# Homes that outlive attention: the first weights and tokens of stage 1 are loaded before attention has ended

## The chip, the cores and the metric

The kernel runs on one core of a Trainium2 chip. The metric is the device time of one execution in microseconds (us), as the median of several runs. One execution was also recorded by the hardware profiler; all rows below come from that recording.

## What is computed

Three parts follow one another, each reading what the one before it wrote:

```python
scores = 1/sqrt(64) * q @ k.T                      # 4 batches, 12 heads, 448 x 448
scores = einsum('bhij,hg->bgij', scores, w_pre)    # heads mixed before the softmax
attn = softmax(scores)
attn = einsum('bhij,hg->bgij', attn, w_post)       # and after it
x = (attn @ v) as 1792 tokens x 768
h = x @ w_in; x = (h - tanh(h)) @ w_out            # d_ff 2048
d, c = softmaxes over columns and rows of x @ phi  # 32 slots, 8 experts
out = c @ experts(d.T @ x)
```

## The kernel before

**Attention** (`talking_heads`) handles 184 slots of up to ten query rows each, numbered 0 to 183. In the loop over slots `s`, even slots run `premix` (product `pm`, line 313), `postmix` of the pair four slots back (product `tm`, line 356, into two PSUM tiles that have no second copy), and `expo` (`e`, line 325); odd slots run `recip`, `norm` (`wk`) and `gather` (copies of `tm` to `aT` on ScalarE, lines 373 and 374). `regroup(s + 4)` (line 304, tile `D`) brings the scores of a coming slot into their place by DMA. Beside them run the key and query transposes, `values` (`vx`, line 395, and its copies to `xs` on VectorE, line 405) and the conversion of the double precision weights `w_in` and `w_out` to fp32 (class `Conversion`, tiles `f64` and `fa`; its last step is an addition on GpSimd, line 71). Every step is written in a fixed order (`manual_schedule`), so the order in the code is the order on each engine's queue.

**Stage 1** (`moe_and_slots`) is a generator, which attention advances with `next(more)`. A unit of weights `w` lies in one half of a tile `rg` or `rgs`, and is split into a high and a low part (`split_w`: ScalarE line 787, VectorE or GpSimd line 788); the tokens `xa` likewise (`split_x`, lines 823 and 824). `save_w` (line 801) stores a split unit to DRAM from ScalarE's DMA queue. `product(t)` is 18 matmuls `hp` (line 840), three for each of six pieces of x. `gate_act`, `gate_first` and `gate_last` then compute `h - tanh(h)` on ScalarE and VectorE. Before `box["go"]`, products 0 and 1 run between attention's last steps; then `step(t)` follows for all others, in four passes over the 16 units.

The seam before: at slot 180 all early tiles of attention are released, and the loads are issued from the queue of SyncE (SP):

```python
    for t in range(4):
        load_w(t)
        if t == 0:
            load_x(0)
    yield
    split_w(0, nc.vector)
    save_w(0)
    idle = bank("h1", [128, 128], "warm")
    for _ in range(5):
        nc.tensor.matmul(idle, lhsT=ident, rhs=ident, start=True, stop=True)
```

The tail of attention then advances the generator after `postmix(180)`, `gather(180)`, `postmix(182)`, `gather(182)`, and after the last three `values`. The DMA of the last `xs` (line 380) is issued from ScalarE.

Of the kernel before, what the change touches and what calls it, by code (L numbers as in the profile page):

```python
# [18 lines left out]
NR = 4  # L19
# [54 lines left out]
class Conversion:  # L74
    def __init__(self, nc, w_in, w_out, wi, wo):
# [6 lines left out]
        self.t = {}  # L82

    def load(self, j):
        f, hf, o = j
        r = self.pool.tile([128, self.CV, 2], I32, tag="f64", name="f64", bufs=self.bufs)
# [46 lines left out]
def talking_heads(tc, ident, q, k, v, w_pre, w_post, xd, box, follow):  # L133
# [18 lines left out]
    cv.pool = er  # L152
    psq = early_stack.enter_context(tc.tile_pool(name="at_psq", bufs=2, space=PSUM))
# [7 lines left out]
    def load_k(b, p):  # L161
        t = er.tile([JP, 2, NR, HD], FP32, tag="kn", name="kn", bufs=NP)
        nc.sync.dma_start(out=t, in_=k[b, 2 * p:2 * p + 2].rearrange("e (p r) d -> p e r d", r=NR))
        nat_k[b, p] = t
# [406 lines left out]
    for a in at.get(("head", -1), []):  # L571
        for f in scores4(*a):
            f()
    halves = []
# [4 lines left out]
    while s < NS:  # L579
# [63 lines left out]
def moe_and_slots(tc, ident, xd, wi, wo, wo4, wis, consts, w1, w2, out, box):  # L643
# [34 lines left out]
    keep = whole.enter_context(tc.tile_pool(name="m_keep", bufs=1, reuse_waits="tile"))  # L678
    rgp = whole.enter_context(tc.tile_pool(name="m_ring", bufs=1, reuse_waits="tile"))
    xap = whole.enter_context(tc.tile_pool(name="m_xa", bufs=1, reuse_waits="tile"))  # L680
    xep = firsts.enter_context(tc.tile_pool(name="m_xe", bufs=1, reuse_waits="tile"))
    ph = psums.enter_context(tc.tile_pool(name="m_h", bufs=1, space=PSUM))
    bank_pool = {"h0": ph, "h1": ph}
# [6 lines left out]

    ceK = keep.tile([128, NBL, NSL], FP32, tag="ceK", name="ceK")
# [4 lines left out]
    rg = rgp.tile([128, 2 * RU], FP32, tag="rg", name="rg")  # L696
    rgs = rgp.tile([128, 2 * RU], FP32, tag="rgs", name="rg")
    xbuf = {0: [xap.tile([128, XW], FP32, tag=f"x{l}", name="xa") for l in range(2)]}
    quad, quad_a, quad_b = [xep.tile([128, FB * NRM], FP32, tag=f"quad{i}", name="quad") for i in range(3)]
    ring = [w.rearrange("p (m h i) -> p m h i", m=2, h=2) for w in (rg[:, :RU], rg[:, RU:], rgs[:, :RU], rgs[:, RU:])]  # L700

    def unit(t):
        return ring[t % 4] if t < THREE else ring[(4, 0, 1)[(t - THREE) % 3]]
# [105 lines left out]
    def load_x(p):  # L809
# [7 lines left out]
        step = KD if p else 2  # L817
        for a in range(0, KD, step):
            nc.sync.dma_start(out=dst[:, a:a + step], in_=xd[p][:, a:a + step])
# [275 lines left out]
    def step(t):  # L1095
# [75 lines left out]
        if b == NPASS - 2 and f == NF - 1:  # L1171
            mem["slow"] = True
            for l in range(2):
                give(xap.tile([128, EXB], FP32, tag=f"x{l}", name="ex"))
# [13 lines left out]
    for t in range(4):  # L1188
# [378 lines left out]
```

## Time and profile before

| what | before |
|---|---|
| time, median of 3 runs | 885.64 us (884.59 to 890.2) |
| the profiled execution | 886.23 us, span 884.5 us |
| busy: PE, DVE, ACT, POOL | 807.9, 556.7, 570.5, 247.7 us |
| granted TensorE clock, mean | 0.988 |
| DMA | 224.53 MB, mean 254 GB/s |

PE is TensorE, DVE VectorE, ACT ScalarE, POOL GpSimd, SP SyncE; "ACTq" and "SPq" are the DMA issues of these engines. In a timeline a row gives the start, the time, the engine, the line, the operation, `out<-in`, shapes and the count; what stands in brackets is the idle time of the engine ahead of it and what ended that. An fp32 matmul of the program stands as two records.

### The profile page before, as it was taken

The numbers are of one execution on the slowest core, as the hardware profiler recorded it, in microseconds if no ns is written. First come the engines' busy times: TensorE is split into PE (matmuls) and PEld (weight loads), VectorE is DVE, ScalarE is ACT, GpSimd is POOL, SyncE is SP. The second block draws the span as 40 slices with busy tenths as digits, with TensorE's granted clock in tenths as the row PEclk, the third lists the DMA queues.
The fourth block names the chain that finished last, engine by engine and source line by source line (L and its number), as shares of the span: only waits on it lengthen the run. The fifth ranks groups of instructions, "written<-read, shape, count | busy, mean of one in ns | idle before, by whom it ended". The sixth has DMA issues, their size and how long they took to land.

```text
span 884.5 us, 28648 instructions
## 1 busy us (share of the span) xinstructions
PE 807.9 (91%) x11790; PEld 570.8 (65%) x11790; DVE 556.7 (63%) x1181; ACT 570.5 (64%) x1345; POOL 247.7 (28%) x428
## 2 busy tenths in 40 slices
PE   8889988799987999899899999999999999999965
PEld 6556665566665667566676667667776786964322
DVE  5357766577666777788456986566765777830104
ACT  4777887687776878798666776546664666821103
POOL 5234344334334444454303452000000003700000
PEclk9999999899999999999999999999999999999988
DMA  9787888768888788785759976678764457899998
GB/s 182 191 234 220 213 236 248 218 190 211 231 253 226 219 206 239 236 254 177 256 176 363 374 260 223 207 316 317 302 215 175 149 179 256 313 359 413 424 392 303
DMA packets 131766, 224.53 MB, mean 254 GB/s; under 512 B 44852, under 2 KB 112436, under 8 KB 128052
## 3 DMA queue, kind: packets, MB, share of 16 engines
q1 hardware_dynamic: 128288, 209.84, 74.8%
q10 hardware_dynamic: 3348, 12.87, 3.7%
q8 instruction: 93, 1.52, 0.7%
q14 instruction: 37, 0.30, 0.1%
HBM read 147.96 MB, written 36.18 MB: 208 GB/s over the span
## 4 chain that ended last, share of the span: by engine, by line
PE 50%; DMA 18%; ACT 13%; DVE 12%; issue 5%; SPq 1%; POOL 1%; ACTq 0%; POOLq 0%; DVEq 0%
PE hp L840 21%; DMA D<-S 7%; DMA ex<-in_moe_w_dram 7%; ACT e L325 6%; PE pm L313 5%; PE sc L279 5%; DVE mx L317 4%; PE vx L395 3%; PE tm L356 3%; PE gt L911 2%; ACT S L287 2%; PE kx L236 2%; PE lgp L995 2%; PE sp L1077 1%; ACT aT L370 1%
## 5 line engine op out<-in xcount | busy, mean ns | idle before, releaser
L325 ACT ACTIVATE e<-pm,mx 128x448 f32<-128x448 f32 x184 | 115.1, 631 | 86.3 <-DVE mx L317 84.9
L840 PE MATMUL hp<-xa,rg 128*128 128x512 f32 x576 | 152.7, 405 | 0.2 <-POOL rg L788 0.2
L317 DVE TENSOR_REDUCE mx<-pm 128x1 f32<-128x448 f32 x184 | 106.1, 618 | 73.5 <-PE pm L313 73.4
L356 PEld LDWEIGHTS tm<-wk,e 64*56 64x56 f32 x5888 | 104.7, 128 | 62.8 <-issue 32.4
L356 PE MATMUL tm<-wk,e 64*56 64x60 f32 x5888 | 113.5, 216 | 13.3 <-issue 7.9
L313 PE MATMUL pm<-D,wpre 64*64 64x448 f32 (+2 forms) x736 | 107.6, 565 | 18.4 <-DMA D<-S 15.2
L840 PEld LDWEIGHTS hp<-xa,rg 128*128 128x128 f32 x576 | 102.3, 188 | 28.9 <-issue 10.5
L287 ACT ACTIVATE S<-sc 120x448 f32<-120x448 f32 (+1 forms) x186 | 91.4, 553 | 4.6 <-PE sc L279 3.0
L279 PE MATMUL sc<-khi,qT 64*120 64x448 f32 (+1 forms) x384 | 83.6, 392 | 9.3 <-DVE xs L405 6.2
L342 POOL TENSOR_SCALAR wk<-wpost,rv 128x60 f32<-128x60 f32 x184 | 86.9, 503 | 16.5 <-DVE rv L335 13.8
L331 POOL TENSOR_SCALAR rv<-ss 128x2 f32<-128x2 f32 x92 | 24.5, 266 | 225.3 <-ACT e L325 194.6
L395 PE MATMUL vx<-aT,vn 128*64 128x120 f32 (+1 forms) x1536 | 83.9, 262 | 2.0 <-ACT S L287 1.3
L797 POOL TENSOR_TENSOR rg<-rg 128x384 fp32r<-128x384 f32 x24 | 23.9, 1012 | 208.8 <-DVE rg L794 205.0
L395 PEld LDWEIGHTS vx<-aT,vn 128*64 128x64 f32 x1536 | 74.7, 137 | 7.2 <-issue 3.0
L860 ACT ACTIVATE sq<-hp 128x512 f32<-128x512 f32 (+1 forms) x62 | 32.9, 530 | 68.0 <-PE hp L840 68.0
L370 ACT ACTIVATE aT<-tm 128x480 f32<-128x480 f32 x144 | 75.8, 593 | 0.1
L871 DVE SCALAR_TENSOR_TENSOR qd<-qd,sq 128x512 f32<-128x512 f32 (+1 forms) x61 | 37.6, 616 | 59.1 <-ACT mk L867 53.7
L840 PE MATMUL hp<-xb,rg 128*128 128x512 f32 x288 | 74.7, 404 | 0.0
L840 PEld LDWEIGHTS hp<-xb,rg 128*128 128x128 f32 x288 | 52.1, 188 | 16.6 <-issue 6.3
L279 PEld LDWEIGHTS sc<-khi,qT 64*120 64x120 f32 (+1 forms) x384 | 45.3, 173 | 26.1 <-PE tm L356 9.4
L71 POOL TENSOR_TENSOR fa<-fa,f 128x384 f32<-128x384 f32 x56 | 57.7, 1030 | 6.4 <-DVE f L66 2.1
L313 PEld LDWEIGHTS pm<-D,wpre 64*64 64x64 f32 (+2 forms) x736 | 23.9, 132 | 51.4 <-DMA D<-S 23.2
(199 smaller groups left out, 1391.3 us busy)
## 6 DMA issues: line engine op xcount, KB each, us to landing
ex<-in_moe_w_dram SPq DMA_DIRECT2D x21, 1536.0 KB
D<-S SPq DMA_DIRECT2D x144, 210.0 KB
rg<-wis SPq DMA_DIRECT2D x36, 768.0 KB
f<-in_moe_w_in_dram SPq DMA_DIRECT2D x32, 384.0 KB
wis<-rg ACTq DMA_DIRECT2D x16, 768.0 KB
f<-in_moe_w_out_dram SPq DMA_DIRECT2D x24, 384.0 KB
rg<-wi SPq DMA_DIRECT2D x19, 384.0 KB
wi<-fa SPq DMA_DIRECT2D x32, 192.0 KB
```

The source lines that it names most:

```text
L71: eng.tensor_tensor(out=out, in0=bits(a), in1=bits(p), op=ALU.add)
L279: nc.tensor.matmul(xs[e][0][:ni], lhsT=qT[n][s, l, p, :ni], rhs=kt[s], start=(i == 0), stop=(i == 2))
L287: nc.scalar.activation(out=dst, in_=xs[e][0][:ni], func=ACTF.Copy)
L313: nc.tensor.matmul(xs[x][64 * i:64 * i + 64], lhsT=wpre[k0:k1], rhs=d[i][k0:k1], start=True, stop=True)
L317: nc.vector.tensor_reduce(out=mx[:, x:x + 1], in_=xs[x], op=ALU.max, axis=AX.X, negate=True)
L325: nc.scalar.activation(out=es[x], in_=xs[x], func=ACTF.Exp, bias=mx[:, x:x + 1], accum_out=ss[:, x:x + 1])
L342: nc.gpsimd.tensor_scalar(out=wk, in0=wpost, scalar1=rv[:, x:x + 1], scalar2=None, op0=ALU.mult)
L356: nc.tensor.matmul(xs[i][64 * z:64 * z + JH, x, c], lhsT=es[x][h, j:j + JH], rhs=wks[x][h], start=True, stop=True)
L370: nc.scalar.activation(out=out[:, :, c0:c0 + m].rearrange("p a (x i) -> p a x i", x=2), in_=x, func=ACTF.Copy)
L395: nc.tensor.matmul(x[64 * e:64 * e + 64, i, :ni], lhsT=nat_v[b, h // NP][:, h % NP, c, :], rhs=a[:, c, h, :ni], start=(c == 0), stop=(c == ...
L840: nc.tensor.matmul(hp, lhsT=r32(w[:, m, hl, cs]), rhs=r32(x_of(b, c, l)), start=(c == 0 and i == 0), stop=(c == KD - 1 and i == 2))
L871: nc.vector.scalar_tensor_tensor(out=qd, in0=qd, scalar=TG_E, in1=sq, op0=ALU.add, op1=ALU.mult)
```

## The change

The tiles of the ring (`rg`, `rgs`) and the tile `xl` for x come from a pool `homes` that is opened outside of both parts. During attention `rgs` holds the natural keys (`kns`) and `xl` four of the five raw buffers of the conversion; `rg` holds nothing. From slot 165 on the generator is advanced at every second slot: four loads of w, then three pieces of x. At slot 182 it splits w unit 0, stores it and splits piece 0 of x; at slot 183 pieces 1 and 2. Products 0 and 1 move one or two advances ahead, and the five warm products are gone.

```diff
+    def place(self, x):
+        n = x.shape[1] // 4
+        self.raw = [x[:, i * n:(i + 1) * n] for i in range(4)]
+        self.raw += [self.pool.tile([128, n], FP32, tag="f64", name="f64", bufs=1)]
     def load(self, j):
-        r = self.pool.tile([128, self.CV, 2], I32, tag="f64", name="f64", bufs=self.bufs)
+        r = self.raw[self.loads % self.bufs].bitcast(I32).rearrange("p (f w) -> p f w", w=2)
+        self.loads += 1
...
+    kns = box["homes"].tile([128, NP * 2 * NR * HD], FP32, tag="rgs", name="kn")
+    cv.place(box["homes"].tile([128, 4 * 2 * cv.CV], FP32, tag="xl", name="f64"))
...
+    first_load = NS - D_AHEAD - 15
...
+        if s == first_load:
+            more = follow()
+        if s >= first_load and (s - first_load) % 2 == 0 and s < first_load + 14:
+            next(more)
         if s == NS - D_AHEAD:
             early_stack.close()
-            more = follow()
+            next(more)
+        if s in (NS - 2, NS - 1):
             next(more)
...
+    for t in range(4):
+        load_first(t)
+        yield
+    xl = rgp.tile([128, XW], FP32, tag="xl", name="xa")
+    for a in range(0, KD, 2):
+        nc.sync.dma_start(
+            out=xl.rearrange("p (a s) -> p a s", a=KD)[:, a:a + 2], in_=xd[0][:, a:a + 2])
+        yield
...
-    for t in range(4):
-        load_w(t)
-        if t == 0:
-            load_x(0)
     yield
     split_w(0, nc.vector)
     save_w(0)
-    idle = bank("h1", [128, 128], "warm")
-    for _ in range(5):
-        nc.tensor.matmul(idle, lhsT=ident, rhs=ident, start=True, stop=True)
-    for i in range(0, KD, 2):
-        for c in range(i, i + 2):
-            split_x(0, c)
-        yield
-        product(0, {}, i, i + 2)
+    split_x(0, 0)
+    yield
+    for c in range(1, KD // 2):
+        split_x(0, c)
+    yield
+    product(0, {}, 0, 2)
+    for c in range(KD // 2, KD):
+        split_x(0, c)
+    yield
+    product(0, {}, 2, 4)
+    yield
+    product(0, {}, 4, KD)
```

ScalarE's queue at slot 182, before: the last exponential, the gather of slot pair 178, then the split and the store of w unit 0.

```order
L325 ACTIVATE e_148,ss_8304<-pm_8263,mx_8268 128x448
L373 ACTIVATE aT_8131<-tm_170 128x48x5
L374 ACTIVATE aT_8131<-tm_170 128x48x4
L373 ACTIVATE aT_8131<-tm_171 128x48x5
L374 ACTIVATE aT_8131<-tm_171 128x48x4
L787 ACTIVATE rg_8222<-rg_8222 128x2x384
L801 DMA wis0_89<-rg_8222 128x1536
L823 ACTIVATE xa_8224<-xa_8225 128x512 x2
```

The same place on ScalarE in the changed kernel (lines are some 30 higher there):

```order
L335 ACTIVATE e_151,ss_8227<-pm_8186,mx_8191 128x448
L816 ACTIVATE rg_7574<-rg_7574 128x2x384
L830 DMA wis0_89<-rg_7574 128x1536
L850 ACTIVATE xa_8155<-xa_7879 128x512
L383 ACTIVATE aT_8067<-tm_173 128x48x5
L384 ACTIVATE aT_8067<-tm_173 128x48x4
L383 ACTIVATE aT_8067<-tm_174 128x48x5
L384 ACTIVATE aT_8067<-tm_174 128x48x4
L850 ACTIVATE xa_8155<-xa_7879 128x512 x5
```

The split of w, its store and the first piece of x have moved ahead of the gather.

VectorE's queue at attention's last values, before (the last pair of copies to `xs`, the split of w unit 2, gate 0):

```order
L405 COPY xs<-vx 128x2x8x9
L405 COPY xs<-vx 128x2x2x8
L788 TENSOR_TENSOR rg<-rg 128x2x384
L871 SCALAR_TENSOR_TENSOR quad<-quad 128x512
L872 SCALAR_TENSOR_TENSOR quad<-quad 128x512
L879 TENSOR_TENSOR g_8453<-hp,g_8453 128x512
L884 SCALAR_TENSOR_TENSOR hp<-quad,hp 128x512
L885 COPY_PREDICATED g_8453<-quad,hp 128x512
```

The same place on VectorE in the changed kernel (splits of w units 1 and 2, gate 0, the first pair of copies):

```order
L817 TENSOR_TENSOR rg<-rg 128x2x384 x2
L898 SCALAR_TENSOR_TENSOR quad<-quad 128x512
L899 SCALAR_TENSOR_TENSOR quad<-quad 128x512
L906 TENSOR_TENSOR g_8366<-hp,g_8366 128x512
L911 SCALAR_TENSOR_TENSOR hp<-quad,hp 128x512
L912 COPY_PREDICATED g_8366<-quad,hp 128x512
L415 COPY xs<-vx 128x2x8x9
L415 COPY xs<-vx 128x2x2x8
```

All six copies to `xs` now stand behind gate 0; before, they stood ahead of it. On TensorE, 12 of product 0's matmuls, then `postmix(182)`, the last 6 and all of product 1 now stand ahead of the last three `values`.

SP's queue at slots 173 to 177, before (regroups `D`, stores of converted weights):

```order
L120 DMA wi15_84<-fa_7646 128x384
L304 DMA D_143<-S_7380 108x1x448
L304 DMA D_144<-S_7380 108x1x448
L304 DMA D_139<-S_7380 108x1x448
L120 DMA wi15_84<-fa_7809 128x384
L304 DMA D_140<-S_7380 108x1x448
```

The same place on SP in the changed kernel:

```order
L127 DMA wi15_84<-fa_7572 128x384
L718 DMA xa_7879<-xd0_65 128x1024
L314 DMA D_146<-S_7307 108x1x448
L314 DMA D_147<-S_7307 108x1x448
L718 DMA xa_7879<-xd0_65 128x1024
L314 DMA D_142<-S_7307 108x1x448
L127 DMA wi15_84<-fa_7739 128x384
```

The first piece of x stands ahead of the regroups of slots 178 and 179. It waits there for GpSimd's addition of the last converted piece, whose raw buffer lies in `xl`.

## Rows read from the trace of the kernel before

**Rows 1.** The page's part 4: shares of the chain that ended last, by engine.

```profile
PE 50%; DMA 18%; ACT 13%; DVE 12%; issue 5%; SPq 1%; POOL 1%; ACTq 0%; POOLq 0%; DVEq 0%
```

**Rows 2.** The chain in order of time, from 560 us: start, us, what.

```profile
804.17 16.60 DMA ex<-in_moe_w_dram
```

**Rows 3.** Timeline of the seam, TensorE: start, us, instructions, idle before them.

```profile
437.48 1.31 PE L356 MATMUL tm<-wk,e 64*56 64x60 f32 x55 [0.20 <-ACT aT L374]
...
441.30 0.36 PE L356 MATMUL tm<-wk,e 64*56 64x60 f32 x9 [2.51 <-issue]
...
441.60 1.38 PE L1197 MATMUL warm<-ident 128*128 128x128 f32 x10
...
442.73 1.64 PE L840 MATMUL hp<-xa,rg 128*128 128x512 f32 x6
...
444.30 1.07 PE L356 MATMUL tm<-wk,e 64*56 64x60 f32 x64
...
448.26 3.86 PE L395 MATMUL vx<-aT,vn 128*64 128x88 f32 x96
452.06 5.73 PE L840 MATMUL hp<-xa,rg 128*128 128x512 f32 x24
...
462.35 0.73 PE L840 MATMUL hp<-xa,rg 128*128 128x512 f32 x2 [0.19 <-POOL rg L788]
```

**Rows 4.** The same timeline, ScalarE, VectorE and GpSimd.

```profile
436.68 0.44 ACT L373 ACTIVATE aT<-tm 128x240 f32<-128x240 f32 x1
...
437.65 0.86 ACT L787 ACTIVATE rg<-rg 128x768 fp32r<-128x768 f32 x1
...
438.54 0.96 DVE L788 TENSOR_TENSOR rg<-rg 128x768 fp32r<-128x768 f32 x1 [0.64 <-ACT rg L787]
439.53 0.35 ACTq L801 DMA_DIRECT2D wis<-rg  x1
...
442.64 2.21 ACT L823 ACTIVATE xa<-xa 128x512 fp32r<-128x512 f32 x4
...
448.71 0.60 ACT L860 ACTIVATE quad<-hp 128x512 f32<-128x512 f32 x1 [1.53 <-PE hp L840]
...
450.44 0.71 ACT L867 ACTIVATE quad<-quad,tlimit 128x512 f32<-128x512 f32 x1
...
452.17 0.49 DVE L405 COPY xs<-vx 128x144 f32<-128x144 f32 x2 [0.74 <-PE vx L395]
452.69 0.62 ACTq L380 DMA_DIRECT2D xd<-xs  x1
453.36 0.85 ACT L787 ACTIVATE rg<-rg 128x768 fp32r<-128x768 f32 x1 [2.20 <-DVE xs L405]
...
455.11 0.68 DVE L871 SCALAR_TENSOR_TENSOR quad<-quad 128x512 f32<-128x512 f32 x1
...
460.45 1.84 POOL L788 TENSOR_TENSOR rg<-rg 128x768 fp32r<-128x768 f32 x1 [22.08 <-ACT rg L787]
```

**Rows 5.** Timelines of regroups: issues on SP, GpSimd's last addition, TensorE's premix.

```profile
41.29 1.68 SPq L304 DMA_DIRECT2D D<-S  x2
...
45.77 0.60 PE L313 MATMUL pm<-D,wpre 64*64 64x448 f32 x3 [2.17 <-DMA D<-S]
...
418.28 3.58 SPq L304 DMA_DIRECT2D D<-S  x3
...
419.91 1.01 POOL L71 TENSOR_TENSOR fa<-fa,f 128x384 f32<-128x384 f32 x1
...
425.76 1.58 PE L313 MATMUL pm<-D,wpre 64*64 64x448 f32 x8 [0.78 <-ACT e L325]
```

**Rows 6.** Windows: length, busy of PE, PEld, DVE, ACT, POOL, PEclk, DMA share, GB/s.

```profile
46.00:50.00 4.00, 4.00 (x82) 3.16 (x75) 2.51 (x6) 2.51 (x7) 0.93 (x3) 0.64 0.83 205
50.00:54.00 4.00, 3.22 (x78) 1.50 (x74) 2.10 (x5) 2.43 (x8) 1.07 (x5) 0.93 1.06 214
...
442.00:444.00 2.00, 2.00 (x15) 1.76 (x14) 0.72 (x3) 2.00 (x7) 0.00 (x0) 1.00 0.71 276
```

More of the change, by code (lines that the diff above doesn't have):

```diff
@@ L161, in load_k @@
     def load_k(b, p):
-        t = er.tile([JP, 2, NR, HD], FP32, tag="kn", name="kn", bufs=NP)
+        n = 2 * NR * HD
+        t = kns[:JP, p * n:(p + 1) * n].rearrange("p (e r d) -> p e r d", e=2, r=NR)
         nc.sync.dma_start(out=t, in_=k[b, 2 * p:2 * p + 2].rearrange("e (p r) d -> p e r d", r=NR))
@@ L677, in moe_and_slots @@
     psums = ExitStack()
[L678 to L683, printed above, removed]
+    rgp = box["homes"]
+    bank_pool = {}
     def bank(tag, shape, name):
@@ L689, in r32, with unit, load_first @@
         return ap.bitcast(F32R)
+    rg = rgp.tile([128, 2 * RU], FP32, tag="rg", name="rg")
+    rgs = rgp.tile([128, 2 * RU], FP32, tag="rgs", name="rg")
+    ring = [w.rearrange("p (m h i) -> p m h i", m=2, h=2) for w in (rg[:, :RU], rg[:, RU:], rgs[:, :RU], rgs[:, RU:])]
+    def unit(t):
+        return ring[t % 4] if t < THREE else ring[(4, 0, 1)[(t - THREE) % 3]]
+    def load_first(t):
+        nc.sync.dma_start(out=unit(t)[:, :, 1], in_=wi[t].rearrange("p (m i) -> p m i", m=2))
+    for t in range(4):
[6 more added lines that the diff above has]
+        yield
+    keep = whole.enter_context(tc.tile_pool(name="m_keep", bufs=1, reuse_waits="tile"))
+    xap = whole.enter_context(tc.tile_pool(name="m_xa", bufs=1, reuse_waits="tile"))
+    xep = firsts.enter_context(tc.tile_pool(name="m_xe", bufs=1, reuse_waits="tile"))
+    ph = psums.enter_context(tc.tile_pool(name="m_h", bufs=1, space=PSUM))
+    bank_pool.update(h0=ph, h1=ph)
     ceK = keep.tile([128, NBL, NSL], FP32, tag="ceK", name="ceK")
@@ L694, in moe_and_slots @@
     wphi = keep.tile([128, NF, NSL], FP32, tag="wphi", name="wphi")
-    rg = rgp.tile([128, 2 * RU], FP32, tag="rg", name="rg")
-    rgs = rgp.tile([128, 2 * RU], FP32, tag="rgs", name="rg")
-    xbuf = {0: [xap.tile([128, XW], FP32, tag=f"x{l}", name="xa") for l in range(2)]}
+    xbuf = {0: [xap.tile([128, XW], FP32, tag="x0", name="xa"), xl]}
     quad, quad_a, quad_b = [xep.tile([128, FB * NRM], FP32, tag=f"quad{i}", name="quad") for i in range(3)]
-    ring = [w.rearrange("p (m h i) -> p m h i", m=2, h=2) for w in (rg[:, :RU], rg[:, RU:], rgs[:, :RU], rgs[:, RU:])]
-    def unit(t):
-        return ring[t % 4] if t < THREE else ring[(4, 0, 1)[(t - THREE) % 3]]
     def by_column(e):
@@ L816, in load_x @@
         dst = dst.rearrange("p (a s) -> p a s", a=KD)
-        step = KD if p else 2
-        for a in range(0, KD, step):
-            nc.sync.dma_start(out=dst[:, a:a + step], in_=xd[p][:, a:a + step])
+        nc.sync.dma_start(out=dst, in_=xd[p])
     def split_x(b, c, eng=nc.vector):
@@ L1172, in step @@
             mem["slow"] = True
-            for l in range(2):
-                give(xap.tile([128, EXB], FP32, tag=f"x{l}", name="ex"))
+            give(xap.tile([128, EXB], FP32, tag="x0", name="ex"))
+            give(rgp.tile([128, EXB], FP32, tag="xl", name="ex"))
         if b == NPASS - 1:
@@ L1533, in fused_kernel @@
     }
+    box["homes"] = ctx.enter_context(tc.tile_pool(name="homes", bufs=1, reuse_waits="tile"))
     with tc.manual_schedule():
```

1 line of the change is left out of this document (added).

## The prediction

> **What bounds the kernel now.** I read the shares of the chain first, to see whether the place that the change touches lies on it, and then the seam from attention to stage 1, engine by engine. TensorE holds half of the chain [rows 1]; the last part, from 804 us on, hangs on the loads of the experts' weights [rows 2]. Those loads are issued at fixed places in TensorE's steps, as homes come free, so a shift of the seam moves them too. I therefore let a microsecond won or lost at the seam count as one at the end, and look only at when TensorE can run step 3 (product 3), which before begins in earnest at 462.35 us, on the heels of GpSimd's split of w unit 3 [rows 3, 4].
>
> At the seam TensorE is the engine in question, and it has three holes. Postmix of slots 180 and 181 begins at 437.48, stops for 2.51 us with only "issue" as the reason, and ends at 441.66; then come the warm products, and product 0 begins at 442.73 [rows 3]. The third is small: 0.19 us for the split of unit 3. So what early loads and the removed products can give is at most about 2.5 + 1.1 + 0.2, plus what better order yields. The question is what is late next.
>
> **The change, part by part.**
>
> *Loads moved ahead of the seam.* Seven loads, 3.1 MB, go from slots 180 and 181 to slots 165 to 177. What they cost at the old place is the queue ahead of the splits; what they cost at the new one is three things. The issues themselves, seven of about half a microsecond to 0.84 [rows 5], stand on SP between regroups which have more than six microseconds to spare (issue at 418.28, use at 425.76) [rows 5]: nothing, as long as that stays. The first piece of x is the exception. It waits for the addition on GpSimd that ends at 420.92 [rows 5], and the regroups of slots 178 and 179 are queued behind it, which were issued from 418.28 on. Now: 420.95, plus 0.84 for the piece's issue, plus 1.68 for two regroups, gives 423.5. An issue of two regroups ended at 42.97 and its data was there at 45.77, 2.8 us later, in a busy stretch [rows 5]; so they land at 426.3, where TensorE wanted them at 425.76. That is 0.5 us late. The bounds are nothing (an idle queue) and the 2.17 us that one regroup cost at 45.77. I take 0.5, since the piece of x ahead of it speaks for the upper side and the empty queue at that time for the lower. TensorE has next to no holes between there and the seam, so it passes on.
>
> *The homes.* Keys and raw buffers lie in slices of one tile instead of tiles of their own. The orders and waits of attention are the same up to slot 165; I cost this at nothing, and nothing has to cover it.
>
> *The split of unit 0, its store and piece 0 of x ahead of the gather of slots 178 and 179.* This is where I expect the gain to go. Before, ScalarE began that gather at 436.68, and postmix of 180, which writes the same two PSUM tiles, could begin 0.8 us later [rows 3, 4]. Now ScalarE does at 436.68: the high part (0.86) until 437.54; the store, which waits for VectorE's low part (0.96) until 438.5 and takes 0.35 to issue; then a quarter of 2.21 for piece 0 [rows 4], until 439.5. That an activation waits behind such an issue is seen at 453.36: ScalarE sat idle 2.20 us until VectorE's last copy let the DMA of `xs` go at 452.69, and the split behind it, whose data had long been there, ran right after that issue [rows 4]. So the gather begins 2.8 us later, and postmix of 180 at 440.3. It ends 1.31 later, at 441.6: the same moment as before, 441.66. The stall of 2.51 us is gone (nothing large is in the queues there now; if it comes back it costs up to 2.51 more), and a wait of 3.0 us, from 437.28, has taken its place.
>
> *The warm products.* Product 0 now begins at 441.6 and not at 442.73: minus 1.1 us on TensorE. The first pieces of x are split by then (ScalarE 0.55 each). Twelve products at 5.73/24 us [rows 3] end at 444.5, postmix of 182 (1.07) at 445.6, product 0 at 447.0 and product 1 at 451.3; then the last values, 3.8 us (448.26 to 452.06) [rows 3], end at 455.1. Step 2 took at most 10.1 - 4.3 = 5.8 us (452.06 to 462.16 holds products 1 and 2) [rows 3], so TensorE would be at step 3 by 460 or 461: one to two microseconds gained, if that were all.
>
> *Gate 0 ahead of the copies to `xs`.* It isn't. ScalarE: gate 0 from 447.1 for 2.44 us (448.71 to 451.15), the gather of 182 some 0.97 (436.68 to 437.65), the high part of unit 2 0.86 [rows 4]: 451.4. VectorE: its low part 0.96, five steps of gate 0 at 0.68, and only then three pairs of copies at 0.49 [rows 4]: 457.2. The DMA of `xs` (0.62) holds ScalarE's queue until 457.8; behind it stand gate 1 (2.44), the high part of unit 3 (0.85), and GpSimd's low part (1.84) [rows 4], which ends at 463.1. Before, this DMA stood at 452.69. Step 3 begins 0.75 us later than before, and TensorE waits there two microseconds or more.
>
> *The clock.* [...] After the 2.51 us at the seam it stayed at 1.00 [rows 3, 6], with the warm products right behind. The changed kernel has a wait of 3.0 us at the same place without them, and a second one at step 3. [...]
> [...]
>
> *Sum.* 0.75 + 0.5 + 1.7 = 2.95 us later. Against the profiled execution (span 884.5, 886.23 in all) that is 889.2; the median of the runs lies 0.6 below it, so 888.6. A difference of under 1% (8.9 us) can hardly be told from no change in this kernel, whose three runs spread over 5.6 us; so this is "no change", on its slow side.
>
> **The rivals.**
>
> *The clock holds* through both waits, as it did after 2.51 us: 885.64 + 1.25 = 886.9. [...]
>
> *It falls twice*, at the seam and at step 3: 890.3. The second wait is shorter than the first, and TensorE works ten microseconds and more between them.
>
> *Faster: the gather isn't held by the store.* If ScalarE took up the gather while the store still waits for VectorE, the gather would begin at 436.68 + 0.86 + 0.55 = 438.1 and postmix of 180 end at 440.2, 1.4 us earlier than in the sum. The DMA of `xs` wouldn't hold gate 1 either, which would then follow gate 0 on VectorE as before; unit 3 would be split by 458, and TensorE itself would set the pace: it is at step 3 by about 459, against 462.2. [...] With 0.5 for the regroups: 882.9. Against it stands the 2.20 us at 453.36 [rows 4].
> [...]
>
> *Slower by over 1%: regroups land late, again and again.* The three pieces of x stand between the last regroups on SP and in the DMA queues. If the regroups of 178, 180 and 182 each land after TensorE has come to them, and each costs the 2.17 us of 45.77 [rows 5], that is 6.0 beyond what the sum has; with a second fall of the clock, 896.3. It decides from the point where a regroup, issued at 423.5, 426 or 429.6, needs over 2.3, 4 and 4 us to land. The 2.8 us measured speak against it for the second and third.
>
> *It doesn't do what it says:* x pieces that land no earlier than the splits want them, and everything as before: 885.6.
>
> **How the numbers follow.** One fall of the clock, as summed: 0.43. The clock holds: 0.20. Two falls: 0.13. Faster: 0.14. Slower by over 1%: 0.05. As before: 0.05. The predicted time is that of the first, 888.6. The range of 882 to 892 takes in the faster rival, whose floor is near 882, the two falls, and the bounds of regroups (2.0) and of a returning stall, though not all of them at once; what is left out is the rival of late regroups and the ends of the others. Faster by over 1%: 0.02, since no case reaches 876.8. Slower by over 1%: 0.06, the regroups and a sum of bad ends. Within 1%: 0.92.
>
> **What would show it.** In the changed kernel's timeline: TensorE idle for about 3 us ahead of postmix of 180, released by ScalarE's `aT`, and no "issue" stall of 2.5 us in it; a granted clock under 1.00 somewhere from 441 to 446; product 0's first twelve matmuls in one run; gate 1's first square on ScalarE after 457 and not at 456.64, behind the DMA of `xs`; GpSimd's split of unit 3 ending past 463, with TensorE waiting for it; premix of 178 released by a regroup. It is wrong if that gather begins before 438.5 (then the faster rival), if TensorE's wait at step 3 is missing, or if more than one premix waits for a regroup.

## The result, and the profile of the changed kernel

The changed kernel takes 896.82 us in the median (893.03 to 901.78, 19 runs), the kernel before 889.28 in the same comparison (883.81 to 895.5, 19 runs): 1.0086 times as long, with an interval of 1.0064 to 1.0107. That is 7.5 us slower, within 1%, where 2.95 were forecast, and 896.8 lies outside the range of 882 to 892. The profiled execution of the changed kernel took 893.12 us (span 891.4).

The seam is best read with three marks in TensorE's timeline: the start of premix of 176, the start of the values just ahead of postmix of 180 (the expectations below call them the third from last), and the first `wt` of step 3. In the kernel before they stand here (start, us, instructions, idle before them):

```profile
423.15 0.98 PE L313 MATMUL pm<-D,wpre 64*64 64x448 f32 x8
...
430.07 0.98 PE L313 MATMUL pm<-D,wpre 64*64 64x448 f32 x8
...
435.42 1.86 PE L395 MATMUL vx<-aT,vn 128*64 128x120 f32 x32
...
462.92 0.49 PE L964 MATMUL wt<-ident,ex 128*128 128x128 f32 x3
```

So the first stretch, the end of attention, is 12.27 us, and the second, from there to step 3, 27.50. The same timeline of the changed kernel, which answers to [rows 3]:

```profile
422.80 0.98 PE L323 MATMUL pm<-D,wpre 64*64 64x448 f32 x8
425.74 0.93 PE L323 MATMUL pm<-D,wpre 64*64 64x448 f32 x2 [1.11 <-DMA D<-S]
427.45 0.60 PE L323 MATMUL pm<-D,wpre 64*64 64x448 f32 x3 [0.78 <-DMA D<-S]
...
430.99 1.10 PE L323 MATMUL pm<-D,wpre 64*64 64x448 f32 x5
...
436.95 1.38 PE L323 MATMUL pm<-D,wpre 64*64 64x448 f32 x5 [1.84 <-DMA D<-S]
...
439.47 1.86 PE L405 MATMUL vx<-aT,vn 128*64 128x120 f32 x32
444.33 1.42 PE L366 MATMUL tm<-wk,e 64*56 64x60 f32 x64 [3.00 <-ACT aT L384]
445.69 3.04 PE L867 MATMUL hp<-xa,rg 128*128 128x512 f32 x12
...
449.65 5.82 PE L867 MATMUL hp<-xa,rg 128*128 128x512 f32 x24
455.40 2.65 PE L405 MATMUL vx<-aT,vn 128*64 128x88 f32 x64
460.22 2.57 PE L405 MATMUL vx<-aT,vn 128*64 128x88 f32 x32 [2.18 <-DVE xs L415]
...
469.20 0.73 PE L867 MATMUL hp<-xa,rg 128*128 128x512 f32 x2 [0.93 <-POOL rg L817]
469.77 0.49 PE L991 MATMUL wt<-ident,ex 128*128 128x128 f32 x3
```

The first stretch has grown to 16.67 us (+4.40) and the second to 30.30 (+2.80): 7.2 us in all, which is the loss at the seam. In the first, the premixes of 178 and 182 wait for their regroups. In the second, four things are to be seen: the wait of 3.00 us for `aT` without a stall on issue, product 0's first twelve in one run, a hole of 2.18 us between the second and the third group of the last values, and a short wait for GpSimd at step 3.

The marks begin at 176, while the first load goes out at slot 165. From the premix of 164 to that of 176 the kernel before took 22.81 us (400.34 to 423.15), with one stall on issue, and the changed kernel 25.42 (397.38 to 422.80), with two. Before:

```profile
410.15 0.37 PE L356 MATMUL tm<-wk,e 64*56 64x60 f32 x10 [0.61 <-issue]
```

and changed:

```profile
404.15 0.95 PE L366 MATMUL tm<-wk,e 64*56 64x60 f32 x53 [1.50 <-issue]
...
410.29 0.37 PE L366 MATMUL tm<-wk,e 64*56 64x60 f32 x10 [2.17 <-issue]
```

Of the kernels of the next section, the one without early loads (homes_only) took 22.79 us there, and the other twelve 22.92 to 26.99. So early loads seem to cost something here too; the last section has what the traces show of these stalls. The times do not show it: swap_old, with the 26.99, is not slower than before. And up to the premix of 164 the fifteen profiles differ by 11.3 us (396.16 to 407.47), so one execution of each settles little.

ScalarE, VectorE and GpSimd in the second stretch, which answer to [rows 4]:

```profile
440.75 0.84 ACT L816 ACTIVATE rg<-rg 128x768 fp32r<-128x768 f32 x1
441.62 0.96 DVE L817 TENSOR_TENSOR rg<-rg 128x768 fp32r<-128x768 f32 x1 [1.18 <-ACT rg L816]
442.61 0.35 ACTq L830 DMA_DIRECT2D wis<-rg  x1
443.01 0.63 ACT L850 ACTIVATE xa<-xa 128x512 fp32r<-128x512 f32 x1 [1.42 <-DVE rg L817]
443.54 0.43 ACT L383 ACTIVATE aT<-tm 128x240 f32<-128x240 f32 x1
...
456.36 0.69 DVE L898 SCALAR_TENSOR_TENSOR quad<-quad 128x512 f32<-128x512 f32 x1
...
459.63 0.78 DVE L415 COPY xs<-vx 128x144 f32<-128x144 f32 x4
462.83 0.48 DVE L415 COPY xs<-vx 128x144 f32<-128x144 f32 x2 [2.42 <-PE vx L405]
463.34 0.62 ACTq L390 DMA_DIRECT2D xd<-xs  x1
464.06 0.60 ACT L887 ACTIVATE quad<-hp 128x512 f32<-128x512 f32 x1 [8.61 <-DVE xs L415]
467.32 1.82 POOL L817 TENSOR_TENSOR rg<-rg 128x768 fp32r<-128x768 f32 x1 [21.88 <-ACT rg L816]
```

ScalarE sits 1.42 us behind the store of unit 0, and the gather of 178 (443.54) behind that. Later VectorE does gate 0 first and the copies to `xs` after it (459.63); the third group of values needs a PSUM bank that these copies empty, so the third pair of copies waits 2.42 us for TensorE, and the DMA of `xs`, gate 1's square (8.61 us of idle on ScalarE) and the split of unit 3 come in a row behind.

The regroups: SP's issues and GpSimd's last addition, which answer to [rows 5]:

```profile
419.56 1.02 POOL L71 TENSOR_TENSOR fa<-fa,f 128x384 f32<-128x384 f32 x1
420.60 0.33 SPq L718 DMA_DIRECT2D xa<-xd  x1
421.02 1.71 SPq L314 DMA_DIRECT2D D<-S  x2
...
429.68 0.72 SPq L718 DMA_DIRECT2D xa<-xd  x1
430.50 1.59 SPq L314 DMA_DIRECT2D D<-S  x2
```

The first piece of x goes out at 420.60, 0.02 after the addition's end. The regroups behind it are issued by 422.73 and used at 425.74 and 427.45, 3.0 and 4.7 us later; those behind the third piece are issued by 432.09 and used at 436.95, 4.9 us later. SP stood still from 417.13 to 420.60, and then issued almost without a gap (0.1 us at most) until 432.09. Windows (length, busy of PE, PEld, DVE, ACT, POOL, granted clock, DMA share, GB/s), which answer to [rows 6]:

```profile
440.00:445.00 5.00, 1.95 (x50) 1.61 (x50) 2.17 (x4) 3.58 (x11) 0.62 (x2) 1.00 0.33 135
445.00:450.00 5.00, 5.00 (x134) 4.03 (x124) 4.49 (x7) 3.95 (x10) 0.44 (x2) 1.00 0.33 101
...
460.00:465.00 5.00, 4.78 (x42) 4.20 (x43) 0.88 (x6) 0.91 (x2) 0.00 (x0) 0.66 0.93 307
```

The clock held behind the wait of 3.00 us and fell behind that of 2.18. On the chain in order of time, the row that answers to [rows 2] is as long as before and 8.42 us later; the end of the span is 6.9 later:

```profile
812.59 16.60 DMA ex<-in_moe_w_dram
```

### The profile page after: what moved, and what is told of

It reads as the page before. It is cut to its first block, busy times and chain, and to the rows that moved or that the text cites. A ratio compares the mean times of both kernels' runs of the same rounds, so it can differ in the third digit from the quotient of the medians.

```text
span 891.4 us, 28623 instructions
## 1 busy us (share of the span) xinstructions
PE 813.5 (91%) x11780; PEld 574.7 (64%) x11780; DVE 556.1 (62%) x1181; ACT 570.5 (64%) x1345; POOL 247.9 (28%) x428
## 4 chain that ended last, share of the span: by engine, by line
PE 52%; DMA 18%; DVE 12%; ACT 11%; issue 5%; POOL 1%; ACTq 0%; SPq 0%; POOLq 0%; DVEq 0%
PE hp L867 21%; DMA D<-S 10%; DMA ex<-in_moe_w_dram 7%; PE pm L323 6%; PE sc L289 5%; ACT e L335 5%; DVE mx L327 4%; PE vx L405 4%; PE tm L366 3%; PE gt L938 2%; ACT S L297 2%; PE kx L246 2%; PE lgp L1022 2%; PE sp L1104 1%; ACT aT L380 1%
## 5 line engine op out<-in xcount | busy, mean ns | idle before, releaser
L366 PEld LDWEIGHTS tm<-wk,e 64*56 64x56 f32 x5888 | 106.6, 128 | 60.3 <-issue 31.1
L323 PE MATMUL pm<-D,wpre 64*64 64x448 f32 (+3 forms) x736 | 112.7, 566 | 17.5 <-DMA D<-S 14.0
L366 PE MATMUL tm<-wk,e 64*56 64x60 f32 x5888 | 115.4, 216 | 13.6 <-issue 6.6
L867 PEld LDWEIGHTS hp<-xa,rg 128*128 128x128 f32 x576 | 102.6, 189 | 30.5 <-issue 10.7
L323 PEld LDWEIGHTS pm<-D,wpre 64*64 64x64 f32 (+3 forms) x736 | 25.6, 132 | 54.1 <-DMA D<-S 24.0
```

What stands on the lines that cost most here:

```text
L323: nc.tensor.matmul(xs[x][64 * i:64 * i + 64], lhsT=wpre[k0:k1], rhs=d[i][k0:k1], start=True, stop=True)
L366: nc.tensor.matmul(xs[i][64 * z:64 * z + JH, x, c], lhsT=es[x][h, j:j + JH], rhs=wks[x][h], start=True, stop=True)
L867: nc.tensor.matmul(hp, lhsT=r32(w[:, m, hl, cs]), rhs=r32(x_of(b, c, l)), start=(c == 0 and i == 0), stop=(c == KD - 1 and i == 2))
```

## The experiments

The theory after the result had two parts: late regroups (4.4 us, because pieces of x stand in front of them) and the new order of the seam (2.8 us). The rivals were: the homes themselves cost something; only the wait for GpSimd makes the regroups late; one place of the order, or the clock, carries the second part. All kernels were timed against the kernel before. The table has the two stretches in the profiled execution of each (us, from the starts of the three marks), their sum beyond the 39.77 of before, and the ratio of times with its interval. "New" and "old" is the order of the seam.

| kernel | loads ahead of slot 180 | seam | marks | first | second | beyond | ratio |
|---|---|---|---|---|---|---|---|
| before | none | old | 423.15, 435.42, 462.92 | 12.27 | 27.50 | 0 | 1 |
| the change | w, x | new | 422.80, 439.47, 469.77 | 16.67 | 30.30 | 7.20 | 1.0086 [1.0064, 1.0107] |
| homes_only | none | old | 419.94, 432.17, 461.32 | 12.23 | 29.15 | 1.61 | 1.0031 [0.9998, 1.0064] |
| x_late | w | new | 424.06, 436.35, 467.10 | 12.29 | 30.75 | 3.27 | 1.0041 [1.001, 1.0072] |
| gather_first | w, x | new, gather earlier | 425.96, 443.93, 472.65 | 17.97 | 28.72 | 6.92 | 1.0081 [1.0047, 1.0114] |
| gate_late | w, x | new, gate 0 later | 424.99, 440.67, 471.39 | 15.68 | 30.72 | 6.63 | 1.009 [1.0053, 1.0126] |
| third_late | w, two pieces of x | new | 424.01, 439.74, 470.00 | 15.73 | 30.26 | 6.22 | 1.0067 [1.004, 1.0095] |
| swapped | x, then w | new | 427.08, 443.07, 471.49 | 15.99 | 28.42 | 4.64 | 1.0099 [1.0063, 1.0134] |
| w_early_old_seam | w | old | 430.42, 445.20, 470.08 | 14.78 | 24.88 | -0.11 | 1.0013 [0.9979, 1.0047] |
| x_late_warm | w | new, warm products | 422.68, 435.71, 464.90 | 13.03 | 29.19 | 2.45 | 1.0061 [1.003, 1.0091] |
| all_early_old_seam | w, x | old | 425.05, 441.01, 466.70 | 15.96 | 25.69 | 1.88 | 1.003 [1.0002, 1.0058] |
| swap_old | x, half of w | old | 425.19, 438.28, 463.53 | 13.09 | 25.25 | -1.43 | 0.9982 [0.9952, 1.0011] |
| x_late_gather | w | new, gather earlier | 423.59, 436.59, 464.79 | 13.00 | 28.20 | 1.43 | 1.0043 [1.0014, 1.0072] |
| x_late_values | w | new, values earlier | 421.90, 434.21, 466.89 | 12.31 | 32.68 | 5.22 | 1.0078 [1.0048, 1.0109] |
| old_seam_no_warm | w | old, no warm products | 427.98, 440.21, 467.45 | 12.23 | 27.24 | -0.30 | 0.9999 [0.996, 1.0037] |

**The homes alone** (homes_only):

```diff
-        if s == first_load:
-            more = follow()
-        if s >= first_load and (s - first_load) % 2 == 0 and s < first_load + 14:
-            next(more)
...
+            more = follow()
```

with the loads in the order of before, and the old seam. 

> The tiles lie in their lasting homes as in the change, but every load, split, product and warm product stands where it stood before. Theory A (regroups held up behind the pieces of x) and theory B (the new order at the seam) both expect the time of before, within 2 us. Rival C, that the new places in SBUF or the shared tiles slow attention itself, expects 3 us or more above before, and a premix of slot 164 that is late by as much.

Measured: 1.0031, an interval that includes 1; the first stretch is that of before, 12.23. TensorE's stall on issue is there as before, and the 1.65 us more in the second stretch go with a clock of 0.85 and 0.81 behind it (435 to 445), where it held before, though the warm products stand there in both:

```profile
438.07 0.36 PE L366 MATMUL tm<-wk,e 64*56 64x60 f32 x9 [2.49 <-issue]
```

Its premix of 164 begins at 397.15, 3.2 us earlier than before, so attention isn't late. The 2.8 us in the median lie between the 2 that the theories allowed and the 3 of the rival: the homes are not shown to cost anything, nor to cost nothing, and most of the loss comes from what is done with them.

**x moved back** (x_late):

```diff
-        if s >= first_load and (s - first_load) % 2 == 0 and s < first_load + 14:
+        if s >= first_load and (s - first_load) % 2 == 0 and s < first_load + 8:
...
-            next(more)
+            for _ in range(4):
+                next(more)
```

> The change, but the three pieces of x are issued at slot 180, behind the last regroup, and not at slots 173 to 177; the four loads of w stay early. Theory A expects 3.5 to 4.5 us less than the change (some 3 us above before), with no premix from slot 178 on waiting for a regroup. Theory B expects the time of the change, within 1 us.

Measured: 1.0041. The first stretch is 12.29, and no premix waits for a regroup: the pieces of x cost the 4.4 us, and the loads of w cost the regroups nothing. The second stretch, 30.75, is still long; its two waits in TensorE's timeline are those of the change, but the clock fell behind both (0.79 and 0.86 from 440 to 450, 0.66 from 460 to 465):

```profile
441.20 1.42 PE L366 MATMUL tm<-wk,e 64*56 64x60 f32 x64 [2.99 <-ACT aT L384]
...
458.67 1.44 PE L405 MATMUL vx<-aT,vn 128*64 128x88 f32 x32 [2.18 <-DVE xs L415]
```

**Which piece of x, and why.** third_late puts only the third piece back:

```diff
-        if s >= first_load and (s - first_load) % 2 == 0 and s < first_load + 14:
+        if s >= first_load and (s - first_load) % 2 == 0 and s < first_load + 12:
...
             next(more)
+            next(more)
```

> The change, with only the third piece of x moved back behind the last regroup. Measured so far: from the premix of 176 to the third from last values TensorE needs 12.27 us in the kernel before, 16.67 in the changed one, 12.29 with all three pieces moved back. If the third piece, which stands right ahead of the last pair of regroups, makes most of the 4.4 us, that stretch comes to 13 to 14 us and the time is near that of all three moved back (ratio 1.003 to 1.006). If it is the wait of the first piece for GpSimd's last addition, at the head of the queue, the stretch stays at 15.5 to 16.7 us and the ratio at 1.008.

swapped gives x a home that nothing used before, loads it first, and puts units 0 and 1 of w, which follow the conversion buffers, last:

```diff
-    cv.place(box["homes"].tile([128, 4 * 2 * cv.CV], FP32, tag="xl", name="f64"))
+    cv.place(box["homes"].tile([128, 4 * 2 * cv.CV], FP32, tag="rg", name="f64"))
...
-    for t in range(4):
-        load_first(t)
-        yield
     xl = rgp.tile([128, XW], FP32, tag="xl", name="xa")
...
+    for t in (2, 3, 0, 1):
+        if t == 0:
+            rg = rgp.tile([128, 2 * RU], FP32, tag="rg", name="rg")
...
+        load_first(t)
+        yield
```

> The change with the homes exchanged: x has a home that nothing used before, and its pieces go out from slot 165 to 169; units 2 and 3 of w_in follow, and units 0 and 1, in the old conversion buffers, go out at slots 175 and 177, by when GpSimd's last addition is over. If the wait for that addition at the head of SP's queue made the regroups late, the stretch from the premix of 176 to the third from last values falls from 16.67 to 12.3 to 13 us (ratio 1.004). If it is the bytes that stand ahead of the regroups, two loads of 0.39 MB stand there still in place of two of 0.52 MB: 14.5 to 16 us (ratio 1.006 to 1.008).

Measured: both first stretches stay long (15.73 and 15.99), at different premixes, and each bears out another rival: 15.73 lies in the 15.5 to 16.7 of the wait for GpSimd, 15.99 in the 14.5 to 16 of the bytes. The ratios are less clear: 1.0067 lies between what the two rivals of third_late said, 1.0099 above what either of swapped did. TensorE in third_late, premix of 178:

```profile
428.22 0.93 PE L323 MATMUL pm<-D,wpre 64*64 64x448 f32 x2 [2.37 <-ACT aT L380]
429.30 0.60 PE L323 MATMUL pm<-D,wpre 64*64 64x448 f32 x3 [0.15 <-DMA D<-S]
```

Its premix of 182 doesn't wait any more, but that of 178 is later than in the change; the name `aT` stands for a copy long done, and what came last was the regroup, to judge by the row behind it. In swapped the premix of 178 is in time, since nothing waits for GpSimd, and that of 182 waits behind a unit of w:

```profile
438.00 0.93 PE L323 MATMUL pm<-D,wpre 64*64 64x448 f32 x2 [0.38 <-DMA D<-S]
440.14 0.66 PE L323 MATMUL pm<-D,wpre 64*64 64x448 f32 x3 [1.21 <-DMA D<-S]
```

So both seem to be at work, as far as one profile of each shows: the first pair is late only where the head of SP's queue waits for GpSimd (with a piece of x ahead of the pair as well), and the last pair only where a load stands ahead of it. What it comes to does not depend much on which: every kernel with a large load in front of a regroup from slot 175 on has 3.4 to 5.7 us more in its first stretch, and those without have 0.8 at most, except w_early_old_seam, where most of the 2.5 us are stalls on issue. Not all of it is the wait for a regroup: in gate_late that wait is 0.49 us, beside stalls on issue of 1.78 and 1.07, and in third_late, swapped, gather_first and all_early_old_seam the clock fell behind the late premix (means of 0.53 to 0.68 over five us).

**Single places of the new order.** gather_first puts the split and store of unit 0 and piece 0 of x behind the gather of 178:

```diff
-        if s in (NS - 2, NS - 1):
+        if s == NS - 1:
+            next(more)
             next(more)
```

> The change, but split and store of w unit 0 and the first pieces of x stand behind the gather of slot 178 on ScalarE. Postmix of slot 180 should start without its wait of 3.0 us. If that wait was the cost, 2.5 to 3 us less than the change. My own sum says that the wait only moves: product 0 needs piece 0 of x, whose low part then comes some 1.5 us later on VectorE, so TensorE waits ahead of product 0 and the time is that of the change, within 1 us.

gate_late puts gate 0 on VectorE behind the copies to `xs`:

```diff
     load_w(5)
+    yield
     gate_first(0)
     gate_last(0)
-    yield
     gate_act(1)
```

> The change, but gate 0 on VectorE stands behind the six copies of the last values, as before the change. Theory B in its narrow form (the third group of values waits 2.2 us for a bank whose copy is queued behind gate 0, and ScalarE's DMA of xs with it) expects 1.5 to 2.5 us less than the change, and no idle time of TensorE between the second and third group of values. If step 3 is held by something else, the time of the change within 1 us.

Neither moved the time (1.0081 and 1.009). In gate_late the hole between the values is gone, and the turn of gate 0's result waits instead. Its second stretch also has a fall of the clock (0.50 and 0.82 from 445 to 455) that the change did not have, so the profile can't tell what the order alone is worth there:

```profile
459.32 3.86 PE L405 MATMUL vx<-aT,vn 128*64 128x88 f32 x96
...
466.99 0.66 PE L938 MATMUL gt<-ident,g 128*128 128x128 f32 x4 [2.22 <-DVE g L912]
```

In gather_first the second stretch is 1.58 shorter than in the change and the first 1.30 longer. x_late_gather repeats that edit without the late regroups. 

> The kernel with x moved back, and the split and store of unit 0 and piece 0 of x behind the gather of slots 178 and 179 instead of ahead of it. The wait of 2.99 us ahead of postmix of 180 goes; product 0 then waits for the first piece of x, 1.1 us. If the gather's place is what the new seam costs, 28.7 us from the third from last values to step 3 in place of 30.75, and a ratio of 1.001 to 1.003; if the wait only changes its place, 30.5 us and 1.004.

Measured: 28.20 in the second stretch against 30.75, and 1.0043 against 1.0041: what the profile shows as won isn't found in the time. The clock stayed at 1.00 from 440 to 450, where the fall in x_late cost 1.75 us of work, so most of the 2.55 may be the clock. Product 0 now waits where postmix did, and the hole in the values stays:

```profile
441.19 3.47 PE L869 MATMUL hp<-xa,rg 128*128 128x512 f32 x12 [1.14 <-ACT xa L852]
...
456.34 1.43 PE L405 MATMUL vx<-aT,vn 128*64 128x88 f32 x32 [2.18 <-DVE xs L415]
```

x_late_values is x_late with the last values ahead of product 1 and gate 0 again:

```diff
         gather(u)
-        next(more)
+        if u < NS - 2:
+            next(more)
     for g in range(3):
         values(NC - 1, g)()
     next(more)
+    next(more)
```

> The kernel with x moved back, and one step of the seam exchanged: the last values and their copies stand ahead of product 1, the split of unit 2 and gate 0 again, as in the kernel before; the gather stays behind the split, the store and piece 0 of x, and there are no warm products. If the values' place is what the new seam costs (the wait of 2.18 us for xs, the late DMA of xs, gate 1 and the split of unit 3 behind it), the three groups of values run in one row, and from the third from last values to step 3 it takes 27 to 28 us instead of 30.75: ratio 1.001 to 1.002. If it is the gather's place and its wait of 2.99 us, or the warm products, 30 us and 1.004 stay.

Measured: the opposite, 1.0078 and 32.68. The three groups do run in one row, but only after a wait of 3.47 us, and at half the clock (0.50 in the window from 450 to 455, 6.53 us instead of 3.86). TensorE:

```profile
439.08 1.42 PE L366 MATMUL tm<-wk,e 64*56 64x60 f32 x64 [3.01 <-ACT aT L384]
...
449.56 6.53 PE L405 MATMUL vx<-aT,vn 128*64 128x88 f32 x96 [3.47 <-ACT aT L384]
```

and ScalarE ahead of it:

```profile
444.73 0.33 ACTq L833 DMA_DIRECT2D wis<-rg  x1
446.13 0.60 ACT L890 ACTIVATE quad<-hp 128x512 f32<-128x512 f32 x1 [2.42 <-PE hp L870]
...
448.48 0.44 ACT L383 ACTIVATE aT<-tm 128x240 f32<-128x240 f32 x1
```

The gather of 182, whose input was done at 444.49, stands behind the store of unit 1 and gate 0, which waited 2.42 us for product 0 on ScalarE.

**The warm products.** x_late_warm is x_late with the five products in the wait ahead of postmix of 180:

```diff
     for c in range(1, KD // 2):
         split_x(0, c)
+    idle = bank("h1", [128, 128], "warm")
+    for _ in range(5):
+        nc.tensor.matmul(idle, lhsT=ident, rhs=ident, start=True, stop=True)
```

> The kernel with x moved back, and the five warm products put into TensorE's wait of 2.99 us ahead of postmix of 180, where they take 2.3 to 2.4 us of it and delay nothing. If the fall of the clock at 440 to 450 us (means 0.79 and 0.86, 1.75 us of work) sets the pace there, it goes: from the third from last values to step 3 29 us instead of 30.75, ratio 1.002 or 1.003. If only the order of the waits does, 30.7 us and 1.004 as before.

Measured: the second stretch is 29.19, near what the clock's part was expected to give, with the clock at 1.00 from 440 to 450; but the time is not better (1.0061, 1.0041 without them), so the fall there was not shown to set it.

**The order as a whole.** w_early_old_seam is x_late with the old seam:

```diff
-    split_x(0, 0)
-    yield
-    for c in range(1, KD // 2):
-        split_x(0, c)
...
+    idle = bank("h1", [128, 128], "warm")
+    for _ in range(5):
+        nc.tensor.matmul(idle, lhsT=ident, rhs=ident, start=True, stop=True)
+    for i in range(0, KD, 2):
+        for c in range(i, i + 2):
+            split_x(0, c)
+        yield
+        product(0, {}, i, i + 2)
```

> The four units of w_in loaded early as in the change, x at slot 180, and from there on the order of the kernel before, warm products included. If the new order of the seam (split and store of unit 0 and x piece 0 ahead of the gather, gate 0 ahead of the copies) is what costs 2 to 3 us in the kernel with x moved back, this one is faster than that by as much: ratio 0.998 to 1.001, with the wait of 2.99 us for aT and that of 2.18 for xs both gone; the stall of 2.5 us on issue is shorter or gone, since 1.5 MB instead of 3.1 go out there. If the early loads themselves cost, the ratio stays at 1.004.

all_early_old_seam is the change itself with the same edit. 

> All seven loads where the change has them, and from slot 180 on the order of the kernel before, warm products included: the fourth cell of a square, beside the change (early x, new seam, ratio 1.0086), x moved back (late x, new seam, 1.0041) and units early with the old seam (late x, old seam, 1.0013). If late regroups and seam order are two separate costs that add, this one is at 1.0013 + 0.0045, so 1.005 to 1.007, with 15.5 to 17 us from the premix of 176 to the third from last values. If the old seam takes the lateness up (its own stall of 2.5 us goes instead), it is at 1.001 to 1.003.

Measured: 1.0013, a little above the 0.998 to 1.001 expected, and 1.003. Beside 1.0041 and 1.0086 that makes a square: the old order is worth 0.0056 (5.0 us) with x early, where the intervals don't touch, and 0.0028 (2.5 us) with x late, where they overlap; x late is worth 0.0045 with the new order and 0.0017 with the old, overlapping in both. By what was put down ahead of the run, 1.003 is the case in which the old seam takes the lateness up (1.001 to 1.003), and not that of two costs that add (1.005 to 1.007): in all_early_old_seam the first stretch is as late as expected, about as long as in swapped, and the second 1.81 shorter than before, without the old stall of 2.51 in its timeline. In w_early_old_seam the second stretch is 2.62 shorter than before and the first 2.51 longer, by stalls like this one in postmix of 178:

```profile
444.51 0.75 PE L366 MATMUL tm<-wk,e 64*56 64x60 f32 x41 [1.48 <-issue]
```

old_seam_no_warm takes the warm products out of it:

```diff
-    idle = bank("h1", [128, 128], "warm")
-    for _ in range(5):
-        nc.tensor.matmul(idle, lhsT=ident, rhs=ident, start=True, stop=True)
     for i in range(0, KD, 2):
```

> Units of w_in early, x at slot 180, the order of the seam of the kernel before, and only the five warm products left out. Moving the gather forward, moving gate 0 back, moving the values forward and putting warm products in have each been tried alone in the new seam, and none brought the time back to that of the old one. Either the warm products are what the old seam has over them: then this one is at 1.004 with the clock under 1.00 between the third from last values and product 1. Or the order as a whole is: then it stays at 1.000 to 1.002, with 24.5 to 26 us from the third from last values to step 3 (24.88 with the warm products), since what TensorE waits for between the postmix and product 0 is the split of x and not the warm products.

Measured: 0.9999, as expected if it is the order and not the products; the interval reaches up to 1.0037, so this is likely rather than shown. The second stretch is not the 24.5 to 26 that was expected with it but 27.24, with a stall on issue of 0.88. The clock did fall without the products (0.69 from 445 to 450), and the time is that of before all the same:

```profile
445.00:450.00 5.00, 4.54 (x72) 3.16 (x73) 3.79 (x6) 4.51 (x13) 0.00 (x0) 0.69 0.45 174
```

**A better version?** swap_old takes the loads of swapped without units 0 and 1, which go out at slot 180, and the old seam:

```diff
-        if s >= first_load and (s - first_load) % 2 == 0 and s < first_load + 14:
+        if s >= first_load and (s - first_load) % 2 == 0 and s < first_load + 10:
...
-            next(more)
+            for _ in range(3):
+                next(more)
```

> A candidate for a version better than both: x into a home of its own from slot 165 to 169, units 2 and 3 of w_in at slots 171 and 173, units 0 and 1 only at slot 180 behind the last regroups but one, and the order of the seam of the kernel before. No load stands in front of a regroup from slot 174 on and none waits for GpSimd, so no premix waits: 12.3 to 13 us from the premix of 176 to the third from last values, or up to 14.8 with stalls on issue. From there to step 3 24.9 us, as with the units early (27.5 before). If both hold, ratio 0.996 to 0.999; if the stalls on issue only move, as with the units early, 1.000 to 1.002.

Measured: 0.9982, with an interval of 0.9952 to 1.0011. It has the shortest seam of all, 1.43 us under that of before, and no premix waits; but it can't be told from the kernel before. Against the change it gives back the whole loss: the two intervals don't touch.

## Why the prediction was wrong

Of the 8.2 us between 888.6 and 896.82, 3.6 are the kernel before: its median was 885.64 in three runs, on which the forecast stands, and 889.28 in nineteen. The other 4.6 are missing in the sum.

**The loads moved ahead: here it failed.** The step took 0.5 us for the regroups of 178 and 179, with bounds of nothing and 2.17, and left the others out; the stretch grew by 4.40. The first pair came to 1.27 (the premix of 180 begins 8.19 us behind that of 176, 6.92 before): more than 0.5, but inside its bounds. The other 3.13 came with the last pair of regroups and behind it, which the sum had at nothing. Two of its numbers were wrong. The landing of 2.8 us came from a pair with a load of 224 KB ahead of it; behind a piece of x, 512 KB, it was 3.0 to 4.9. And the slack: the prediction has the last pair issued at 429.6, with 4 us to land; it was issued by 432.09, and TensorE came to it at 435.11, 3.0 us later. The issues on SP, which it took to cost nothing, are why: SP never made up for its wait for GpSimd's addition. (The "more than six microseconds to spare" count from the start of a row of three issues that lasts 3.58 us [rows 5].) The rival "regroups land late, again and again" had the mechanism, at a chance of 0.05; the mark that the prediction set for it, more than one premix that waits for a regroup, is in the trace. That its 896.3 comes near the 896.82 is luck: it stands 10.7 us over the 885.64 from which it was worked out, and 7.5 were measured. Two of its three premixes were late and not all, and the clock's second fall was not part of it. x_late shows the term's size: with x back, the first stretch is 12.29. The step also had nothing for what early loads may do to TensorE at their new place, the stalls of 1.50 and 2.17 us between 164 and 176; whether they cost time is open.

**The homes** at nothing: not contradicted (1.0031, with 1 in the interval), but not shown either.

**The split, the store and piece 0 ahead of the gather**: right in the trace nearly to the tenth. Its gather begins 2.8 us behind the split's start as summed (443.54 after 440.75), TensorE waits 3.00 where 3.0 was said, and the old stall on issue isn't there. The rival that the gather isn't held by the store fell: ScalarE sat idle for 1.42 us behind the store and for 8.61 behind the DMA of `xs`. Nothing behind the waiting issue started in either place.

**The warm products** and the chain behind them: right. With the seam's shift of 4.05 us the last values were to begin at 455.35, and began at 455.40.

**Gate 0 ahead of the copies**: the direction and the whole chain were right (copies, DMA of `xs`, gate 1, split of unit 3, TensorE waiting at step 3), the size was not. The step has the three pairs of copies in a row and gate 1 behind 457.8; counted with the seam's shift of 4.05 us the DMA should have been out by 461.85, and was at 463.96. It left out that TensorE can't write the third group of values before a copy has emptied a bank: 2.18 us of wait, then 2.57 for the group, most of it with the clock at half (0.50 from 461 to 463).

**The clock**: one fall was taken, at the first wait; one came, at the second. The 1.7 us of the sum are an estimate from [rows 6], whose means of 0.64 and 0.93 are that much short of eight us at 1.00; the profile of the change doesn't show them at the wait they were put down for, where the clock was 1.00 from 440 to 450. At the second wait they are not a term of their own, since the fall lies inside the chain just told, where it shows as 2.57 us for the third group and 2.11 for the six matmuls behind it, against 1.29 (a third of the 3.86 in gate_late) and 1.64 [rows 3] at the full clock: 1.75, so the size was right and the place wrong. What a fall costs in the timed runs stays open: x_late_warm has one fewer than x_late and isn't faster, old_seam_no_warm has one and isn't slower than the kernel before. Nor did the length of the wait tell whether a fall follows: after the same wait of 3.0 us the clock held in the change (1.00 from 440 to 450), in third_late (the same) and in x_late_values (1.00 from 435 to 445), and fell in x_late (0.79 and 0.86 from 440 to 450) and gate_late (0.50 and 0.82 from 445 to 455).

**The sum of the second stretch** was 0.75 + 1.7 = 2.45, and 2.80 was measured: near, by partly other terms, so partly by luck. From the mark of step 3 to the end the profiles of both kernels take 421.6 us, which bears out that a microsecond at the seam counts as one at the end. That the 7.2 us of the seam come so near the 7.5 of the medians is luck in part, since in these two profiles the stretch from 164 to 176 was 2.6 longer as well, and all ahead of it 3.0 shorter. What stays open is why moving the gather alone gains 1.6 to 2.6 us in the second stretch of a profile and nothing in the times; the second of these is partly the clock.

## What to carry to other kernels

A load that is issued earlier goes in front of something else in its queue: list the small, urgent transfers behind it, take their slack from the changed order and not from the old one, and take their landing time from a transfer that had such a load ahead of it (here 3.0 to 4.9 us behind 512 KB, against 2.8 behind 224 KB). An early load whose home still waits for another engine belongs behind the urgent transfers, not at the head of their queue. Where several queues hand each other work, as at this seam, one step moved alone tends to move the wait: the gather, gate 0, the values and the warm products, each edited alone, gained nothing in time; only the whole order did, clear of noise where x was early.

## What the runs showed of the hardware

The stalls that the trace calls "issue" stand in the middle of a row of equal matmuls, with no releaser. The profiles of the kernel before and of the change have fourteen of over 0.15 us (0.18 to 2.51), eight and six, all between 114 us and step 3, some of them long in the kernel before too (2.29 us at 362.51). All fourteen stand at the same place, to one, in every 256 of TensorE's instructions (weight loads, matmuls and those of its sequencer, in order of time). The page of the kernel before, part 3, has this among its DMA queues, with its packets, MB and share:

```profile
q8 instruction: 93, 1.52, 0.7%
```

In the DMA records of the two traces, each of the fourteen stalls ends 1.29 to 1.62 us after the end of a packet of this queue. The packet had started 3.2 us (before) and 3.5 us (change), in the median, after TensorE passed the last such place, against 1.7 and 1.6 at the other places from 20 to 480 us (65 in each trace). At the 2.51 us of the kernel before it was 4.1, among the loads of slot 180; at the 1.50 and 2.17 of the change 4.7 and 3.3, among the early loads.

What TensorE waits for in these stalls was not shown, and that it is the loads that bring them on is the author's estimate from these times. The stalls go only loosely with the bytes that are loaded at slot 180: 2.51 and 2.49 us with 3.1 MB (before, homes_only); 2.11 in two parts, 0.88, 0.77 in two parts, 0.32 or none with half of it (w_early_old_seam, old_seam_no_warm, x_late_gather, x_late_warm; x_late and x_late_values); 0.23 and 0.24 with a quarter (swap_old); with nothing, none in the change, swapped and all_early_old_seam, 0.73 in two parts in gather_first, and in gate_late 1.78 and 1.07 in the first stretch. So a stall without a releaser may be one of the costs of a load, wherever the load is put, but no run here settles it.
